# Sparse attention and a GELU layer on one core: the three local jobs of a tile share their score step and their value step

## The chip, the core and the metric

The kernel runs on one core of a Trainium2 chip. The metric is the device time of one execution in microseconds (us). The core's engines are named as the profile names them: PE multiplies matrices (PEld loads its weights), DVE does elementwise work and reductions, ACT does activations and copies, POOL fills and builds masks, SP issues the DMAs. All five run side by side, each through a list of its own, and wait for each other by semaphores.

## The reference

Attention over 8 batches, 8 heads, 576 positions and 64 channels; the first four heads see a window of 32 positions (local), the last four see every 32nd position (strided). Its output, laid out as 4608 tokens of 512 channels, goes through a layer of width 2048 with GELU.

```python
scores = scale * np.matmul(q, k.transpose(0, 1, 3, 2))
rel = pos[:, None] - pos[None, :]
mask_local = (rel >= 0) & (rel < stride)                   # heads 0-3, stride 32
mask_strided = (rel >= 0) & (pos[None, :] % stride == pos[:, None] % stride)   # heads 4-7
attn = softmax(np.where(mask, scores, -1e9))
x = (attn @ v).transpose(0, 2, 1, 3).reshape(B * S, H * D)  # 4608 x 512
h = x @ w_in                                                # 512 x 2048
out = (0.5 * h * (1 + erf(h / sqrt(2)))) @ w_out            # 2048 x 512
```

## The kernel before

**Tiles and steps.** The tokens are cut into 12 tiles of 384, and the layer's width into 16 pieces of 128 (`NF`). A step n handles one piece of one tile: tile n // 16, piece n % 16, 192 steps in all. In a step `ffn_h(n)` does 12 matmuls of 128x384 into one of two PSUM banks `H` (lines L598, L599, L600: each operand is a high and a low part, and three of the four products are taken); `ffn_g(n)` applies GELU on ACT (L607), casts to `gh` on ACT (L609) and subtracts on DVE to get `gl` (L611); `ffn_o(n - 2)` does the 9 matmuls of 128x512 of the step two before (L637, L638, L639) into the banks `O0`, `O1`, `O2`. With two `H` banks, the matmuls H of step n + 2 can begin only when `gl` of step n is done.

**Where x comes from.** The x of a tile (`xh`, `xl`) must be complete when its first step begins. Half of its channels come from the strided heads, worked almost wholly on DVE: products with row sums (L473), a small softmax, then multiply-adds (L515) and a transpose (L523). The other half come from the local heads, in jobs of 128 tokens and four heads, three to a tile (`JPT`). Jobs 0 to 5 (tiles 0 and 1) run in the opening, written out as the list `START`, along with the loading and splitting of the weights and the steps 0 to 15. Jobs 6 to 35 are `band_job`s, and this change is about them.

**A band job** is a generator with seven parts:

- part 0, PE: the scores, 16 matmuls in tiles of 64x32 of the array (L287; 32 records in a trace), half into a PSUM bank `S0`, half into `S1`
- part 1, DVE: mask and row extreme of each of four heads (L301) into a buffer `P`, of which there are two
- part 2, ACT: four exponentials with row sums (L305) into a buffer `PT`
- part 3, DVE and SP: sum, reciprocal, product and 32x32 transpose (L308 to L311), then 8 DMAs that put the blocks into one of three `band` tiles (L316)
- part 4, PE: the values, 8 matmuls in tiles of 96x64 (L324; 16 records in a trace) into a bank `X`
- parts 5 and 6, ACT and DVE: `xh` (L231) and `xl` (L233), then the load of the queries and keys of the job three later

**What sets the order.** In the main loop (steps 16 to 191 and what follows) the order of PE and ACT is the written one, as `step(n)` calls the parts. The orders of DVE, SP and POOL are laid down when the program is built, by the scheduling layer's own reckoning of when rows become ready; on the chip they are then fixed. `PULSES` is a table of 31 steps: 16, 20, 24, then for each later tile three steps (four before, two after and seven after the start of the tile ahead of it), and a last one. At a pulse the values of the job before and the scores of this job stand together, ahead of the step's matmuls H; part 2 follows one step later and part 3 two steps later.

## Time and profile before

| | |
|---|---|
| runs, us | 904.08, 905.25, 905.47 (median 905.25) |
| profiled execution, us | 902.33 |
| its span, first to last instruction, us | 900.6 |
| mean granted clock of TensorE | 0.982 |
| busy, share of the span | PE 97%, PEld 86%, DVE 80%, ACT 49%, POOL 2% |

The profile is one execution seen by the hardware profiler. Its groups give a line's instructions with their busy time and mean duration; its timeline gives instructions in order of time, like ones merged (x16 is sixteen of them, from the first one's start to the last one's end); in brackets stands how long the engine sat idle before it and what ended that. Matmuls overlap, so the pace of PE is read from start to start, not from durations.

### The profile page before, as it was taken

The page shows a single profiled execution, that of the slowest core. Times are in us where ns is not written, and L with a number is a line of the kernel's source. Part 1 is how long each engine was busy: PE and PEld are TensorE (multiplying, and loading weights), DVE is VectorE, ACT ScalarE, POOL GpSimd, SP SyncE. Part 2 cuts the span into 40 slices and gives each one's busy share as a digit, 9 for nine tenths or more (in the row PEclk, how much of TensorE's full clock was granted, in tenths as well). Part 3 has the DMA queues.
Part 4 walks back from the last instruction along what each step waited for, and adds up shares of the span by engine and source line. Part 5 has one row for each costly group of instructions (what it writes and reads, how often), then busy time and mean ns, then how long its engine had stood idle before and what let it go on. Part 6 is the DMA issues. An engine that isn't in the chain of part 4 may idle for free.

```text
span 900.6 us, 19161 instructions
## 1 busy us (share of the span) xinstructions
PE 869.3 (97%) x5948; PEld 772.4 (86%) x5948; DVE 716.2 (80%) x4894; ACT 443.5 (49%) x969; POOL 16.4 (2%) x86
## 2 busy tenths in 40 slices
PE   5599979999999999999999999999999999999998
PEld 4488868888888898888888888888888888889997
DVE  6899988787898899986998996988969899475110
ACT  6899643534544455445544445445453544443222
POOL 4000000000000000000000000000000000000000
PEclk9699998999999999999999999999999999999999
DMA  9992111312112112212121121113112200100001
GB/s 319 361 360 74 51 57 36 101 46 75 30 60 66 31 57 74 75 58 65 30 77 63 57 78 61 32 57 110 32 30 88 70 7 17 59 7 0 36 1 36
DMA packets 33399, 66.27 MB, mean 74 GB/s; under 512 B 6416, under 2 KB 15376, under 8 KB 31248
## 3 DMA queue, kind: packets, MB, share of 16 engines
q1 hardware_dynamic: 33296, 65.04, 22.2%
q8 instruction: 47, 0.77, 0.4%
q14 instruction: 56, 0.46, 0.2%
HBM read 51.64 MB, written 9.44 MB: 68 GB/s over the span
## 4 chain that ended last, share of the span: by engine, by line
PE 92%; ACT 3%; DMA 3%; SPq 1%; issue 0%; DVE 0%
PE H L598 15%; PE O L639 15%; PE O L638 15%; PE H L600 15%; PE H L599 14%; PE O L637 14%; PE X_L L324 2%; DMA ws<-in_w_dram 2%; PE S_L L287 1%; DMA vl<-in_vl_dram 1%; ACT w L160 1%; ACT ws L152 1%; ACT ws L146 0%; SPq L316 0%; ACT L607 0%
## 5 line engine op out<-in xcount | busy, mean ns | idle before, releaser
L607 ACT ACTIVATE H<-H 128x384 f32<-128x384 f32 x192 | 91.3, 476 | 374.5 <-PE H L600 347.3
L598 PE MATMUL H<-xh,w 128*128 128x384 f32 x768 | 264.3, 344 | 4.1 <-DVE gl L611 2.9
L599 PE MATMUL H<-xl,w 128*128 128x384 f32 x768 | 259.8, 338 | 0.7 <-DVE xl L233 0.7
L600 PE MATMUL H<-xh,w 128*128 128x384 f32 x768 | 260.4, 339 | 0.0
L515 DVE SCALAR_TENSOR_TENSOR acc<-sv,sc,acc 128x64 f32<-128x64 f32 x1158 | 248.3, 276 | 0.7
L639 PE MATMUL O<-w,gl 128*128 128x512 f32 x576 | 228.5, 397 | 0.0
L638 PE MATMUL O<-w,gh 128*128 128x512 f32 x576 | 227.8, 396 | 0.0
L637 PE MATMUL O<-w,gh 128*128 128x512 f32 x576 | 225.1, 391 | 0.0
L473 DVE CUSTOM_DVE_ANT_0 junk<-sq,sk 128x64 f32<-128x64 f32 x1290 | 204.3, 219 | 2.1 <-DMA sk<-in_ks_dram 2.1
L611 DVE TENSOR_TENSOR gl<-H,gh 128x384 fp32r<-128x384 f32 x192 | 105.6, 551 | 110.3 <-ACT gh L609 110.2
L598 PEld LDWEIGHTS H<-xh,w 128*128 128x128 f32 x768 | 145.4, 189 | 15.1 <-DVE gl L611 3.8
L599 PEld LDWEIGHTS H<-xl,w 128*128 128x128 f32 x768 | 145.6, 190 | 7.6 <-DVE xl L233 1.1
L600 PEld LDWEIGHTS H<-xh,w 128*128 128x128 f32 x768 | 145.5, 189 | 0.0
L639 PEld LDWEIGHTS O<-w,gl 128*128 128x128 f32 x576 | 108.3, 188 | 23.3
L638 PEld LDWEIGHTS O<-w,gh 128*128 128x128 f32 x576 | 108.4, 188 | 18.3
L637 PEld LDWEIGHTS O<-w,gh 128*128 128x128 f32 x576 | 108.7, 189 | 17.6
L473 DVE DVE_READ_ACCUMULATOR2_ANT sc<- 128x1 f32 x1290 | 106.4, 82 | 0.0
L609 ACT CAST gh<-H 128x384 fp32r<-128x384 f32 x192 | 92.2, 480 | 6.0
L607 ACT ACT_TABLE_LOAD x41 | 52.6, 1283 | 0.9 <-issue 0.2
L483 ACT ACT_TABLE_LOAD x35 | 44.9, 1283 | 0.6
L305 ACT ACTIVATE PT_L<-P_L,nm_L 128x64 f32<-128x64 f32 x120 | 39.9, 333 | 0.0
L231 ACT CAST xh<-X_L 128x256 fp32r<-128x256 f32 x30 | 11.2, 372 | 38.9 <-PE X_L L324 38.7
(106 smaller groups left out, 522.8 us busy)
## 6 DMA issues: line engine op xcount, KB each, us to landing
ws<-in_w_dram SPq DMA_DIRECT2D x16, 1024.0 KB, 14.8
qk<-in_qk_dram SPq DMA_DIRECT2D x36, 320.0 KB, 3.9
out_dram<-ob SPq DMA_DIRECT2D x34, 256.0 KB, 2.7
vl<-in_vl_dram SPq DMA_DIRECT2D x36, 192.0 KB, 2.8
sk<-in_ks_dram SPq DMA_DIRECT2D x8, 576.0 KB, 4.5
sv<-in_vs_dram SPq DMA_DIRECT2D x8, 576.0 KB, 3.8
band<-PT_L SPq DMA_DIRECT2D x240, 16.0 KB, 1.8
sq<-in_qs_dram SPq DMA_DIRECT2D x4, 576.0 KB, 3.6
```

Of the source, the lines that this page charges most:

```text
L473: nc.vector.tensor_tensor_reduce(junk, sq[vi, "q"][:, r0 + r, :], sq[vi, "k"][:, c, :], 1.0, 0.0, ALU.mult, ALU.add, ss[u][:, r, c:c + 1])
L483: exps.append((u, lambda: nc.scalar.activation(s, s, AF.Exp, scale=SC)))
L515: nc.vector.scalar_tensor_tensor(acc[:, r, :], sq[vi, "v"][:, c, :], wgt, acc[:, r, :], ALU.mult, ALU.add)
L598: nc.tensor.matmul(hp, w1[f][:, 0, c, :], xh[:, c, :], start=(c == 0), stop=False)
L599: nc.tensor.matmul(hp, w1[f][:, 0, c, :], xl[:, c, :], start=False, stop=False)
L600: nc.tensor.matmul(hp, w1[f][:, 1, c, :], xh[:, c, :], start=False, stop=(c == NC - 1))
L607: nc.scalar.activation(hp, hp, AF.Gelu)
L609: nc.scalar.copy(gh, hp)
L611: nc.vector.tensor_tensor(gl, hp, gh.bitcast(F32), ALU.subtract)
L637: nc.tensor.matmul(o, gh[:, sl], w2[f][:, 0, :], start=(f == 0), stop=False)
L638: nc.tensor.matmul(o, gh[:, sl], w2[f][:, 1, :], start=False, stop=False)
L639: nc.tensor.matmul(o, gl[:, sl], w2[f][:, 0, :], start=False, stop=(f == NF - 1))
```

## The change

The three band jobs of a tile take their scores in one visit of PE and their values in another. `SCORES` and `VALUES` are steps after the start of the tile ahead: at step 2 the parts 0 of the three jobs, then their parts 1; at step 12 their parts 4, then 5 and 6. The softmaxes stay apart: part 2 and part 3 of job i come 2i + 1 and 2i + 2 steps after the scores. So there are ten visits for scores (18, 34, ... 162) and ten for values (28, 44, ... 172), where there were 31 pulses. The three jobs' scores lie side by side in one pair of banks (128 columns each), and their values in `X` (jobs 0 and 1) and in the bank `S0` (job 2). Nothing else is changed; the buffers `P` and `PT` stay two each, the `band` tiles three.

```diff
-    def band_job(x, bt):
+    def band_job(x, bt, sx):
         QB = STRIDE
-        s = [ps_a.tile([P, DM], F32, name=f"S{j}_L{x}", tag=f"S{j}") for j in range(2)]
+        i = x % JPT
+        if i == 0:
+            sx["s"] = [ps_a.tile([P, DM], F32, name=f"S{j}_L{x}", tag=f"S{j}") for j in range(2)]
+        s = [t[:, i * P:(i + 1) * P] for t in sx["s"]]
...
-        xp = ps_a.tile([P, DM], F32, name=f"X_L{x}", tag="X")
-        xv = xp[:, 0:N2 * P].rearrange("p (r q) -> p r q", r=N2)
+        if i % 2 == 0:
+            sx["x"] = ps_a.tile([P, DM], F32, name=f"X_L{x}", tag="X" if i == 0 else "S0")
+        xv = sx["x"][:, i % 2 * N2 * P:(i % 2 + 1) * N2 * P].rearrange("p (r q) -> p r q", r=N2)
...
-    PULSES = [NB, NB + 4, NB + 8] + [ready[t - 1] + o for t in range(3, NTILE) for o in (-4, 2, 7)]
-    PULSES.append(ready[NTILE - 1] - 4)
+    SCORES, VALUES = 2, 12
+    score_at = {ready[t - 1] + SCORES: t for t in range(2, NTILE)}
+    value_at = {ready[t - 1] + VALUES: t for t in range(2, NTILE)}
...
+    def visit(n):
+        for i in range(JPT):
+            for d, p in ((1, 2), (2, 3)):
+                t = score_at.get(n - 2 * i - d)
+                if t is not None:
+                    if p == 2:
+                        flush_exps(NU)
+                    part(t * JPT + i, p)
+        if n in score_at:
+            for p in (0, 1):
+                for i in range(JPT):
+                    part(score_at[n] * JPT + i, p)
+        if n in value_at:
+            for ps in ((4,), (5, 6)):
+                for i in range(JPT):
+                    part(value_at[n] * JPT + i, *ps)
...
     def step(n):
...
-        before(n)
-        pulse(n)
+        visit(n)
```

The lists of the two built programs show what moves. Names carry the job or the step: `S0_L7` is bank S0 of job 7, `H_20` and `gl_34` belong to steps 20 and 34. Lines from L320 on stand four higher after the change, those between L280 and L317 three.

On PE, before, at step 20 (the second pulse): the end of O of step 17, the values of job 6, and the first scores of job 7.

```order
L638 MATMUL O_1_2_1644<-w_1_584,gh_17_1589 128x512
L639 MATMUL O_1_2_1644<-w_1_584,gl_17_1590 128x512
L324 MATMUL X_L6_1723<-band_1443,vl_6_775 64x64 x8
L287 MATMUL S0_L7_1734<-qk_7_1092 32x64
L287 MATMUL S1_L7_1735<-qk_7_1092 32x64
```

On PE after the change, at step 28: the values of jobs 6, 7 and 8 in one visit, with no scores behind them. The scores of the three (48 rows that alternate between S0 and S1) stand at step 18, right behind H of step 17.

```order
L642 MATMUL O_1_2_1678<-w_9_920,gh_25_2141 128x512
L643 MATMUL O_1_2_1678<-w_9_920,gl_25_2142 128x512
L328 MATMUL X_L6_2254<-band_1443,vl_6_775 64x64 x8
L328 MATMUL X_L6_2254<-band_1443,vl_7_1068 64x64 x8
L328 MATMUL X_L8_2275<-band_1443,vl_8_1347 64x64 x8
L602 MATMUL H_28_2312<-xh_1_826,w_12_1111 128x384
```

The first values have moved from step 20, four steps after their job's scores, to step 28, ten steps after; the pair of values and scores in one visit is gone.

On DVE after the change, behind `gl` of the score step 34: the masks of jobs 9 and 10 stand ahead of these rows, those of job 11 (the third of its tile) here.

```order
L615 TENSOR_TENSOR gl_34_2708<-H_34_2694,gh_34_2707 128x384
L519 SCALAR_TENSOR_TENSOR acc_9_2519<-sv_4_1441,sc_9_1962,acc_9_2519 128x64
L503 TENSOR_REDUCE z_10_96<-sc_10_2352 128x2
L519 SCALAR_TENSOR_TENSOR acc_9_2519<-sv_4_1441,sc_9_1962,acc_9_2519 128x64
L509 TENSOR_SCALAR z_10_96<-z_10_96 128x2
L519 SCALAR_TENSOR_TENSOR acc_9_2519<-sv_4_1441,sc_9_1962,acc_9_2519 128x64
L510 RECIPROCAL z_10_96<-z_10_96 128x2
L304 ISA P_L11_2670,nm_L11_2672<-S0_L9_2602,bmaskNone_89 128x64
```

With two buffers `P`, the third job's masks write the first job's buffer, so they wait for the first job's exponentials on ACT, which stand there behind GELU and cast of step 34; before, the masks of a job waited for its scores alone.

On DVE after the change, at the head of what stands between `gl` of step 133 and that of step 134 (36 rows in all, 23 of L519 by their counts, 9 products L477, a job's product and transpose, one transpose L527, one `xl`).

```order
L615 TENSOR_TENSOR gl_133_9216<-H_133_9202,gh_133_9215 128x384
L519 SCALAR_TENSOR_TENSOR acc_32_9444<-sv_9_8622,sc_32_8859,acc_32_9444 128x64 x2
L313 TENSOR_TENSOR PT_L28_8993<-PT_L28_8993,rs_L28_8996 128x256
L519 SCALAR_TENSOR_TENSOR acc_31_9038<-sv_9_8622,sc_31_8624,acc_31_9038 128x64 x3
L519 SCALAR_TENSOR_TENSOR acc_32_9444<-sv_9_8622,sc_32_8859,acc_32_9444 128x64 x2
L314 STREAM_TRANSPOSE PT_L28_8993<-PT_L28_8993 128x256
```

The softmax of job 28, the second of tile 9, has come here from another step, and two units of strided work stand interleaved with it.

## The prediction

> **What bounds the kernel now.** I read the page first: which engine is busy, and which makes up the chain that ended last.

> ```profile
> span 900.6 us, 19161 instructions
> PE 869.3 (97%) x5948; PEld 772.4 (86%) x5948; DVE 716.2 (80%) x4894; ACT 443.5 (49%) x969; POOL 16.4 (2%) x86
> PE 92%; ACT 3%; DMA 3%; SPq 1%; issue 0%; DVE 0%
> ```

> PE holds 92% of the chain. A busy PE says little of its pace, so I go to the timeline of PE and read starts. First a bare step, then a pulse of two jobs:

> ```profile
> 305.83 0.33 PE L598 MATMUL H<-xh,w 128*128 128x384 f32 x1
> 306.00 0.34 PE L599 MATMUL H<-xl,w 128*128 128x384 f32 x1
> 309.79 0.39 PE L639 MATMUL O<-w,gl 128*128 128x512 f32 x1
> 310.02 0.33 PE L598 MATMUL H<-xh,w 128*128 128x384 f32 x1
> ...
> 313.97 0.40 PE L639 MATMUL O<-w,gl 128*128 128x512 f32 x1
> 314.30 0.69 PE L324 MATMUL X_L<-band,vl 96*64 96x64 f32 x16
> 314.92 0.45 PE L287 MATMUL S_L<-qk 64*32 64x64 f32 x32
> 315.30 0.44 PE L598 MATMUL H<-xh,w 128*128 128x384 f32 x1
> 315.58 0.34 PE L599 MATMUL H<-xl,w 128*128 128x384 f32 x1
> ```

> A step takes 4.19 us (305.83 to 310.02); H follows H after 0.17, and anything follows O after 0.23. At the pulse 0.33 goes by before the values, 0.62 from them to the scores, 0.38 from these to H, and 0.28 to the second H: 1.61, where 0.40 would stand without it. **A pulse costs PE 1.21 us.** The same figures stand at every pulse from 155 us on, and nothing else slows PE there. The stretch before holds three extra losses:

> ```profile
> 108.76 0.39 PE L637 MATMUL O<-w,gh 128*128 128x512 f32 x1
> ...
> 111.06 0.39 PE L638 MATMUL O<-w,gh 128*128 128x512 f32 x1
> 111.38 0.30 PE L287 MATMUL S_L<-qk 64*32 64x64 f32 x2
> 111.61 0.50 PE L639 MATMUL O<-w,gl 128*128 128x512 f32 x1
> ...
> 116.66 0.44 PE L598 MATMUL H<-xh,w 128*128 128x384 f32 x1
> ...
> 124.88 0.40 PE L639 MATMUL O<-w,gl 128*128 128x512 f32 x1
> 125.85 0.45 PE L598 MATMUL H<-xh,w 128*128 128x384 f32 x1 [0.58 <-DVE gl L611]
> 126.14 0.34 PE L599 MATMUL H<-xl,w 128*128 128x384 f32 x1
> ...
> 129.92 0.40 PE L639 MATMUL O<-w,gl 128*128 128x512 f32 x1
> 132.37 0.34 PE L324 MATMUL X_L<-band,vl 96*64 96x64 f32 x4 [2.05 <-DMA band<-PT_L]
> 134.76 0.91 PE L324 MATMUL X_L<-band,vl 96*64 96x64 f32 x12 [2.05 <-DMA band<-PT_L]
> 136.21 0.69 PE L598 MATMUL H<-xh,w 128*128 128x384 f32 x1
> ```

> - The first job's scores come in four pieces among the matmuls O (one shows at 111.38). From 108.76 to 116.66 stand 27 O, 27 x 0.23 = 6.21 of 7.90 us; with the 0.11 that the second H loses at every return (0.28 less 0.17): **1.80**.
> - At 125.85 H waits for `gl`: 0.97 instead of 0.23, and 0.29 instead of 0.17: **0.86**.
> - At step 20 the first values wait twice for the band DMAs. From 129.92 to 136.21 go 6.29 us, against 1.33 at the pulse above: 4.96. Then the clock falls, as windows of the four steps behind this pulse and behind the next show (each from the first H to the last O):

> ```profile
> core 0: us, PE busy (x) PEld busy (x) DVE busy (x) ACT busy (x) POOL busy (x), PEclk, DMA share, GB/s
> ...
> 136.20:155.00 18.80, 18.80 (x92) 17.16 (x84) 16.91 (x150) 8.25 (x20) 0.13 (x1) 0.87 0.14 37
> 156.30:172.90 16.60, 16.60 (x97) 15.08 (x84) 14.07 (x84) 8.08 (x20) 0.11 (x1) 1.00 0.34 112
> ```

> The granted clock was 0.87 instead of 1.00 and the four steps took 2.20 more: with the wait **7.16**.

> [...]

> **The sum before.** 29 pulses with both kinds at 1.21 make 35.1; the last, values alone, 1.21 - 0.38 = 0.83; the three losses 9.8. PE spends **45.7 us** on band jobs and what they provoke, over its bare steps.

> **The change part by part.** *The visits of PE.* In a group, the starts span its length less one matmul's time. L324 lasts 0.69 us with 222 ns for one, so 0.47 over 15 intervals, 31 ns each; L287 0.45 with 216 ns, 0.23 over 31, 7.5 ns each (medians from the lines' own rows):

> ```profile
> L287 PE MATMUL S_L<-qk x960: 216/216/313, 111.4 to 786.7; 64*32 64x64 f32 x192
> ...
> L324 PE MATMUL X_L<-band,vl x480: 222/222/366, 132.4 to 808.5; 96*64 96x64 f32 x160
> ```

> A visit of scores for three jobs is 0.33 + 0.38 for the first, 64 more at 7.5 ns = 0.48, 0.28 at the end, less 0.40: 1.07. A visit of values is 0.33 + 0.62, 32 more at 31 ns = 1.00, 0.28, less 0.40: 1.83. Together 2.90 a tile, 29.0 for ten tiles. The other bound charges each job the whole 0.38 or 0.62, with no gain inside a visit: 1.35 + 2.07 = 3.42, or 34.2. I take 29.0, since the rows inside a group are the nearest to what is added.

> [...]

> *The start.* The first scores stand behind H of step 17 in one piece, so the 1.80 goes into the visit already counted. The order between H and O there changes too; H of step 18 no longer follows two H at once, so `gl` has O and a visit more time, and the 0.86 goes. The first values stand eight steps later. The last of the three softmaxes ends in step 24, its 8 DMAs were issued in 5.37 us (row below), and four steps of 4.19 are left for them. So the 7.16 goes, clock included. What is late next is `gl` on DVE in steps 16 to 21.

> ```profile
> 105.80 0.22 DVE L473 CUSTOM_DVE_ANT_0 junk<-sq,sk 128x64 f32<-128x64 f32 x1
> ...
> 105.95 0.22 DVE L473 CUSTOM_DVE_ANT_0 junk<-sq,sk 128x64 f32<-128x64 f32 x1
> ...
> 111.24 0.55 DVE L611 TENSOR_TENSOR gl<-H,gh 128x384 fp32r<-128x384 f32 x1
> ...
> 128.03 5.37 SPq L316 DMA_DIRECT2D band<-PT_L  x8
> ...
> 303.71 2.63 DVE L515 SCALAR_TENSOR_TENSOR acc<-sv,sc,acc 128x64 f32<-128x64 f32 x13
> ```

> On DVE a product takes 0.15 from start to start, a multiply-add 2.63 / 13 = 0.20. At such paces the list has 5.4, 3.4, 4.6 and 4.9 us of rows from `gl` of step 15 (111.24) to those of steps 16, 17, 18 and 19, which brings the last to 129.5; three short waits on ACT, some 0.6 each, to 131.3. PE, from 108.76 through 27 O, two H and the visit, reaches H of step 18 at 120.2 and H of step 21 at 132.8. So `gl` of step 19 ends about 0.9 us before it is needed, the others earlier. I cost this at nothing; if the cover is gone by more than 2 us, the clock goes too.

> *The third masks, and step 134.* The slack of `gl` in the long run of steps is this (two rows of the timeline, two groups):

> ```profile
> 304.45 0.48 ACT L609 CAST gh<-H 128x384 fp32r<-128x384 f32 x1
> 306.26 0.55 DVE L611 TENSOR_TENSOR gl<-H,gh 128x384 fp32r<-128x384 f32 x1
> ...
> L305 ACT ACTIVATE PT_L<-P_L,nm_L 128x64 f32<-128x64 f32 x120 | 39.9, 333 | 0.0
> L483 ACT ACT_TABLE_LOAD x35 | 44.9, 1283 | 0.6
> ```

> `gh` of step 57 was done at 304.93, `gl` began 1.33 later, and H of step 59 began at 310.02; `gl` could have begun 4.5 us after `gh`. The third job's masks now wait for four exponentials behind `gh`: a table load 1.28, a strided exponential, four at 0.33, some 2.8 us. Queued behind them on DVE are the rest of that step's strided rows and the next `gl`. Masks and rows come to about 3.4 us, so that `gl` begins 6.2 after this `gh`, 2.0 after its own, which comes a step of 4.19 later: inside 4.5. Cost nothing. Between `gl` of steps 133 and 134, though, the list has 23 multiply-adds at 0.20, 9 products at 0.15, and four larger rows beside `gl`: 7.6 us for a step of 4.19. That adds 3.4 to the lateness with which `gl` of step 133 begins. With 1.33, as above, it is 4.7; with twice that, three steps behind a score visit, 6.1; against 4.5. H of step 136 then waits 0.2 to 1.6 us; I charge 0.8 (bounds 0 and 1.6). The list of ACT has 14 more table loads (96 for 82), 18 us, some in front of a GELU; ACT is 49% busy, and 1.28 us of delay is inside the same slack. The loads of queries and keys wait on SP for the scores and come sixteen steps before they are needed; they are not on the path.

> After: 29.0 + 0.8 = 29.8; **gain 45.7 - 29.8 = 15.9 us**. The profiled execution, 902.33 (2.92 below the median), would take 886.4; carried over to the median of the runs, 905.25 - 15.9 = **889.4**.

> **Rivals.**

> - *Each job keeps its own drain* inside a visit: 34.2 instead of 29.0, 894.6. For it: only groups of one job are traced. Against: pieces of 31 and 7.5 ns do not know of jobs. 0.10.
> - *The start stays late*: `gl` takes the place of the band DMAs around steps 19 to 21, stalls PE by about 5 us and halves the clock: 889.4 + 7.2 = 896.6. For it: the cover of 0.9 and the 0.58 wait at 125.85. 0.13.
> - *DVE late in many tiles*, some 0.6 us at each score visit: 895.4. For it DVE's 93.88 busy of 100 us in its fullest stretch; against it 4.5 us of slack. 0.10.

> ```profile
> 300.00:400.00 100.00, 100.00 (x671) 89.27 (x670) 93.88 (x662) 46.64 (x106) 0.64 (x5) 1.00 0.17 55
> ```

> - *Slower*: DVE stands at the third job's masks until the first job's exponentials are through, and `gl` and with it H stop in all ten score steps. It decides from `gl` 4.5 us after `gh`; to eat 15.9 it must be 1.6 us past that each time, so 2.0 would give 889.4 + 20 = 909.4. By the sum above `gl` is some 2 us late, not 6.1. 0.04.
> - *No change*: the gains of the start show in the profiled execution only and drains stay too: about 904. 0.03.

> **How the numbers follow.** The forecast holds 0.60, with its own range 886.6 to 892.2 (0.2 us a tile either way in the visits, 0 to 1.6 at step 136). The range of 8 in 10 takes in the drains, the late DVE and the late start: 886.6 to 896.6. A measurement of this kernel tells about 0.2%, 1.8 us, from no change: faster 0.92, same 0.04, slower 0.04.

> **What would show it.** Right: ten stretches of 1.2 us from the last O to H with 96 score records in them, and ten of 1.95 with 48 value records; a clock of 1.00 from 110 us on; no wait for the band DMAs; at most a short wait of H for `gl` near step 136. Wrong: values that start a new 0.15 us gap at every job; PE waiting for `gl` at 130 us with the clock below 1; waits of H for `gl` that recur every sixteen steps; waits of the masks for ACT above 4 us.

## The result, and the profile after

| | before | after |
|---|---|---|
| first set of runs, median (lowest to highest), us | 905.15 (904.08 to 905.47), 4 runs | 889.27 (887.55 to 891.09), 4 runs |
| ratio, 95% interval | | 0.9827 [0.9803, 0.9850] |
| second set, median, us | 902.71, 17 runs | 889.88 (887.86 to 892.37), 6 runs |
| ratio, 95% interval | | 0.9862 [0.9838, 0.9886] |
| profiled execution, us | 902.33 | 890.20 |
| its span, us | 900.6 | 888.4 |

The kernel became faster by 15.9 us in the first set and by 12.8 us in the second. The page of the kernel after, with its clock row over 40 slices of the span:

```profile
span 888.4 us, 19181 instructions
PE 860.2 (97%) x5948; PEld 771.0 (87%) x5948; DVE 714.1 (80%) x4894; ACT 461.2 (52%) x983; POOL 16.3 (2%) x86
PEclk9699999999999999999999999999999999999999
PE 91%; DVE 4%; DMA 3%; ACT 1%; SPq 0%; issue 0%; DVEq 0%
```

PE still makes the chain, and its clock is 0.9 or more in every slice after the second. The stretch that held the start's losses, as a window of the kernel after (per engine the busy time, then the granted clock, DMA's share and GB/s):

```profile
core 0: us, PE busy (x) PEld busy (x) DVE busy (x) ACT busy (x) POOL busy (x), PEclk, DMA share, GB/s
110.00:155.00 45.00, 45.00 (x317) 40.42 (x316) 43.82 (x411) 27.78 (x63) 0.28 (x2) 1.00 0.19 60
```

No gap of PE and a clock of 1.00 stand there. The timeline of the kernel after, in order: a values visit, a score visit, and what goes on near step 134 on DVE, ACT and PE:

```profile
162.94 0.40 PE L643 MATMUL O<-w,gl 128*128 128x512 f32 x1
163.27 1.62 PE L328 MATMUL X_L<-band,vl 96*64 96x64 f32 x48
164.82 0.44 PE L602 MATMUL H<-xh,w 128*128 128x384 f32 x1
165.10 0.33 PE L603 MATMUL H<-xl,w 128*128 128x384 f32 x1
...
189.81 0.40 PE L643 MATMUL O<-w,gl 128*128 128x512 f32 x1
190.14 1.17 PE L290 MATMUL S_L<-qk 64*32 64x64 f32 x96
191.24 0.45 PE L602 MATMUL H<-xh,w 128*128 128x384 f32 x1
...
629.58 0.57 DVE L615 TENSOR_TENSOR gl<-H,gh 128x384 fp32r<-128x384 f32 x1
...
634.73 0.41 ACT L231 CAST xh<-xs 128x256 fp32r<-128x256 f32 x1 [6.40 <-DVE xs L527]
...
635.54 0.48 ACT L613 CAST gh<-H 128x384 fp32r<-128x384 f32 x1
...
636.50 0.40 PE L643 MATMUL O<-w,gl 128*128 128x512 f32 x1
...
637.19 0.57 DVE L615 TENSOR_TENSOR gl<-H,gh 128x384 fp32r<-128x384 f32 x1
...
637.82 0.44 PE L602 MATMUL H<-xh,w 128*128 128x384 f32 x1 [0.93 <-DVE gl L615]
```

A values visit loses 1.88 + 0.28 - 0.40 = 1.76 us (forecast 1.83), a score visit 1.43 + 0.28 - 0.40 = 1.31 (forecast 1.07): 3.07 a tile instead of 2.90. H of step 136 waits once: 1.32 + 0.28 - 0.40 = 1.20 (forecast 0 to 1.6, charged 0.8).

To compare whole runs, all excess of a start over the bare pace (0.17 us behind H, 0.23 behind O; unrounded 0.174 and 0.231) that is larger than 0.05 us is added up, from the first O behind H of step 15 to the last O. This is **PE's loss**: 45.5 us before, which the prediction put at 45.7, and 31.9 after, which it put at 29.8. The gain of PE's starts is 13.6 us, not 15.9. From outside, the first O to the last took 896.29 - 108.76 = 787.5 us before and 884.13 - 109.62 = 774.5 after: 13.0 less (the other 0.6 us lies in excesses under 0.05). So the gain that the prediction summed was 2.3 us too large, and that 889.4 lies 0.1 us from the first set's median is luck. The profiled execution after took 890.2, not the forecast 886.4. Of these 3.8 us, 2.3 are the smaller gain of PE's starts, 0.6 the excesses under 0.05, and 0.9 stand ahead of the first O counted (109.62 after, 108.76 before), ahead of every visit that the change moves.

### The profile page after: what moved, and what is told of

It reads as the page before. It is cut to its first block, busy times and chain, and to the rows that moved or that the text cites. A ratio compares the mean times of both kernels' runs of the same rounds, so it can differ in the third digit from the quotient of the medians.

```text
span 888.4 us, 19181 instructions
## 1 busy us (share of the span) xinstructions
PE 860.2 (97%) x5948; PEld 771.0 (87%) x5948; DVE 714.1 (80%) x4894; ACT 461.2 (52%) x983; POOL 16.3 (2%) x86
## 4 chain that ended last, share of the span: by engine, by line
PE 91%; DVE 4%; DMA 3%; ACT 1%; SPq 0%; issue 0%; DVEq 0%
PE H L602 15%; PE O L642 15%; PE H L604 15%; PE O L643 15%; PE H L603 15%; PE O L641 14%; DMA ws<-in_w_dram 2%; PE X_L L328 2%; DMA vl<-in_vl_dram 1%; PE S_L L290 1%; DVE acc L519 1%; DVE junk L477 1%; DVE ws L154 0%; DVE w L164 0%; DVE ws L156 0%
## 5 line engine op out<-in xcount | busy, mean ns | idle before, releaser
L611 ACT ACTIVATE H<-H 128x384 f32<-128x384 f32 x192 | 91.4, 476 | 352.8 <-PE H L604 315.6
L519 DVE SCALAR_TENSOR_TENSOR acc<-sv,sc,acc 128x64 f32<-128x64 f32 x1158 | 258.3, 287 | 0.6
L477 DVE CUSTOM_DVE_ANT_0 junk<-sq,sk 128x64 f32<-128x64 f32 x1290 | 214.5, 228 | 6.3 <-DMA sk<-in_ks_dram 6.2
L615 DVE TENSOR_TENSOR gl<-H,gh 128x384 fp32r<-128x384 f32 x192 | 107.4, 560 | 113.1 <-ACT gh L613 112.1
L477 DVE DVE_READ_ACCUMULATOR2_ANT sc<- 128x1 f32 x1290 | 118.8, 92 | 0.0
L611 ACT ACT_TABLE_LOAD x48 | 61.6, 1283 | 1.1 <-issue 0.3
L487 ACT ACT_TABLE_LOAD x35 | 44.9, 1283 | 0.6
L517 DVE TENSOR_SCALAR acc<-sv,sc 128x64 f32<-128x64 f32 x132 | 25.9, 253 | 0.5 <-DMA sv<-in_vs_dram 0.2
```

The costliest lines, as they stand in the source:

```text
L477: nc.vector.tensor_tensor_reduce(junk, sq[vi, "q"][:, r0 + r, :], sq[vi, "k"][:, c, :], 1.0, 0.0, ALU.mult, ALU.add, ss[u][:, r, c:c + 1])
L487: exps.append((u, lambda: nc.scalar.activation(s, s, AF.Exp, scale=SC)))
L519: nc.vector.scalar_tensor_tensor(acc[:, r, :], sq[vi, "v"][:, c, :], wgt, acc[:, r, :], ALU.mult, ALU.add)
L611: nc.scalar.activation(hp, hp, AF.Gelu)
L615: nc.vector.tensor_tensor(gl, hp, gh.bitcast(F32), ALU.subtract)
```

## The experiments

Each kernel is compared with runs of the kernel before on the same chip; "loss" is PE's loss as above. It leaves out what stands ahead of the first O counted, and that stretch is not the same everywhere: in the profiled executions this O begins between 108.24 us (third masks free) and 112.38 us (first values late).

| kernel | median, us | ratio to before, 95% | loss, us |
|---|---|---|---|
| first values late | 896.34 | 0.9933 [0.9910, 0.9955] | 38.6 |
| clean start | 894.63 | 0.9917 [0.9897, 0.9936] | 37.7 |
| old start, shared visits | 900.03 | 0.9971 [0.9959, 0.9984] | 41.7 |
| scores single | 896.43 | 0.9924 [0.9897, 0.9951] | 37.1 |
| scores 1 + 2 | 892.68 | 0.9890 [0.9866, 0.9914] | 35.2 |
| scores mixed | 889.87 | 0.9857 [0.9834, 0.9879] | 31.9 |
| values single | 898.74 | 0.9942 [0.9918, 0.9965] | 38.8 |
| third masks free | 889.55 | 0.9848 [0.9828, 0.9869] | 31.9 |
| xh behind | 889.04 | 0.9842 [0.9827, 0.9858] | 31.2 |
| one visit | 901.40 | 0.9972 [0.9957, 0.9986] | 41.4 |
| one visit, xh behind | 894.53 | 0.9900 [0.9878, 0.9921] | 37.1 |

### The changed kernel again

> The changed kernel once more, unedited, for a tighter interval and as the yardstick of the other kernels of this set. If the gain is the 15.9 us that the prediction summed, the median lies near 889.4 and the ratio near 0.982. The two profiled executions differ by 12.1 us only, and the itemized losses of PE by 13.6 (45.5 before, 31.9 after); if these are the truer figures, the median lies 12 to 14 us below that of before, 891 to 893.

889.88 for 902.71: 12.8 less, loss 31.9. As a difference, this set bears out the second statement and the first set the first (the medians of before differ too, by 2.4 us). The intervals of the two ratios overlap from 0.9838 to 0.9850 only, and the traces' 13.6 us (0.985) stands at the edge of that.

### First values late

The kernel before, with the first values taken out of the pulse of step 20.

```diff
-            part(x - 1, 4)
+            if x - 1 != J0:
+                part(x - 1, 4)
             part(x, 0)
-            part(x - 1, 5, 6)
+            if x - 1 != J0:
+                part(x - 1, 5, 6)
             part(x, 1)
+        if n == NB + 7:
+            part(J0, 4, 5, 6)
```

> The kernel before, with one edit: the values of job 6 stand by themselves at step 23 and no longer at step 20; all else is as before, so the visits of PE keep their old form. My theory: the two waits for the band DMAs (4.96 us) and the fall of the clock behind them (2.20 us) go; the visit at step 20 keeps only scores (0.59 us by 0.33 + 0.38 + 0.28 - 0.40), the one at step 23 only values (0.83), together 0.21 more than one pulse at 1.21. So 6.95 us less than before, near 898.2. Rival 1: the wait goes, but the clock falls in these steps all the same: 4.75 less, near 900.4. Rival 2: the wait stood in the profiled execution only, or the product gl takes its place: no gain, near 905.

Timeline of this kernel, the scores at step 20 and the values at step 23, and its window over these steps:

```profile
133.56 0.40 PE L639 MATMUL O<-w,gl 128*128 128x512 f32 x1
133.89 0.45 PE L287 MATMUL S_L<-qk 64*32 64x64 f32 x32
134.27 0.44 PE L598 MATMUL H<-xh,w 128*128 128x384 f32 x1
...
146.69 0.40 PE L639 MATMUL O<-w,gl 128*128 128x512 f32 x1
147.01 0.69 PE L324 MATMUL X_L<-band,vl 96*64 96x64 f32 x16
147.63 0.44 PE L598 MATMUL H<-xh,w 128*128 128x384 f32 x1
```

```profile
133.80:150.00 16.20, 16.20 (x125) 14.50 (x125) 16.20 (x158) 7.79 (x19) 0.00 (x0) 1.00 0.14 35
```

Scores alone lose 0.71 + 0.28 - 0.40 = 0.59, values alone 0.94 + 0.28 - 0.40 = 0.82. The waits are gone and the clock is 1.00. The loss fell by 6.9 us (forecast 6.95), the median by 6.4: the start's 7.16 were real, clock included. The interval of the ratio alone, 4.1 to 8.1 us, would not tell this from the 4.75 of rival 1; the clock of 1.00 in the window does.

### Clean start

The same edit, and the first scores two steps later.

```diff
-    PULSES = [NB, NB + 4, NB + 8] + [ready[t - 1] + o for t in range(3, NTILE) for o in (-4, 2, 7)]
+    PULSES = [NB + 2, NB + 4, NB + 8] + [ready[t - 1] + o for t in range(3, NTILE) for o in (-4, 2, 7)]
```

> The edit of the kernel before (values of job 6 at step 23), and also the first scores at step 18 instead of 16. My theory: the scores no longer cut up the matmuls O behind H of step 15 (1.80 us less, 0.59 for a visit of scores at step 18) and H of step 18 no longer waits for gl (0.86 less): 6.95 + 1.80 - 0.59 + 0.86 = 9.0 us less than before, near 896.1. Rival: the masks and the softmax of two jobs, now two steps apart, hold gl up on DVE and PE waits in steps 20 to 24: less than 7 us gained, above 898.

The four pieces and the wait of step 18 went, but at step 24 the values of job 7 meet their band DMA. PE, with less lost ahead, is there 2.1 us sooner (37.6 us behind the first O counted; 39.6 in the kernel first values late), while the issue of these DMAs begins 0.6 us later (32.61 for 32.05) and lasts until 147.32, with the visit at 147.34:

```profile
147.02 0.40 PE L639 MATMUL O<-w,gl 128*128 128x512 f32 x1
147.34 0.34 PE L324 MATMUL X_L<-band,vl 96*64 96x64 f32 x4
148.65 0.57 PE L324 MATMUL X_L<-band,vl 96*64 96x64 f32 x12 [0.97 <-DMA band<-PT_L]
...
149.53 0.44 PE L598 MATMUL H<-xh,w 128*128 128x384 f32 x1
```

This visit loses 2.51 + 0.28 - 0.40 = 2.39 instead of 1.21. So 9.0 - 1.2 = 7.8 us were to be had; the loss fell by 7.8, the median by 8.1.

### Old start, shared visits

The changed kernel with jobs 6 to 8 on the pulses 16, 20, 24 and 28.

```diff
...
-    score_at = {ready[t - 1] + SCORES: t for t in range(2, NTILE)}
-    value_at = {ready[t - 1] + VALUES: t for t in range(2, NTILE)}
+    score_at = {ready[t - 1] + SCORES: t for t in range(3, NTILE)}
+    value_at = {ready[t - 1] + VALUES: t for t in range(3, NTILE)}
...
+        first = {NB: 2 * JPT, NB + 4: 2 * JPT + 1, NB + 8: 2 * JPT + 2}
...
+        if n in (NB + 4, NB + 8, NB + 12):
+            part(first[n - 4], 4)
+        if n in first:
+            part(first[n], 0)
...
```

> The changed kernel, with the three jobs of the first tile (6 to 8) put back on the pulses 16, 20, 24 and 28, each with scores and values as before; the nine later tiles keep the shared visits. My theory: the start's losses come back (1.80, 0.86 and 7.16 us) with two pulses at 1.21 and values alone at 0.83, 13.1 in all, and one tile's two visits (1.31 + 1.75 = 3.06 measured) go: 10.0 us more than the changed kernel, 899 to 901. So what the shared visits of nine tiles are worth by themselves is 9 x (3 x 1.21 - 3.06) = 5.1 us. Rival: the visits are worth more than PE's starts show, and the start less: 896 or lower.

The band waits are back in this kernel's timeline:

```profile
132.84 0.34 PE L327 MATMUL X_L<-band,vl 96*64 96x64 f32 x4 [1.96 <-DMA band<-PT_L]
135.35 0.91 PE L327 MATMUL X_L<-band,vl 96*64 96x64 f32 x12 [2.17 <-DMA band<-PT_L]
```

It is 10.2 us slower than the changed kernel in the same set (forecast 10.0), and 2.7 faster than before. The loss fell by 3.8 from before: nine tiles at 3 x 1.21 - 3.07 = 0.56 are 5.0, less the stall of 1.2 near step 136, which stands here too. **Some 10 us of the gain come from the start, some 4 from all the shared visits, the stall near step 136 taken off.**

### Scores single, scores 1 + 2, scores mixed

The changed kernel with its scores split over three visits (scores single, the first diff), over two (scores 1 + 2; the same lines go), or in another order within one (scores mixed: half jobs in turn).

```diff
-        if n in score_at:
-            for p in (0, 1):
-                for i in range(JPT):
-                    part(score_at[n] * JPT + i, p)
+        for i in range(JPT):
+            if n - 2 * i in score_at:
+                part(score_at[n - 2 * i] * JPT + i, 0, 1)
```

```diff
+        if n in score_at:
+            part(score_at[n] * JPT, 0, 1)
+        if n - 2 in score_at:
+            for p in (0, 1):
+                for i in (1, 2):
+                    part(score_at[n - 2] * JPT + i, p)
```

```diff
         for h in range(0, HL, 2):
...
-        yield
+            yield
...
+            for _ in range(2):
+                for x in xs:
+                    next(local[x][0])
```

> The changed kernel, with the scores of the three jobs of a tile taken in three visits, two steps apart (steps 2, 4 and 6 behind the start of the tile ahead); the values still share one. Nothing else moves on PE. A visit of one job's scores alone lost 0.48 + 0.11 = 0.59 us in the kernel before with the late first values. My theory (entry and exit are paid per visit): 3 x 0.59 = 1.77 a tile for 1.31, 4.6 us more than the changed kernel, near 894.5; PE shows 32 records a visit, 7.5 ns apart. Rival (each job keeps its own drain within a shared visit, so a split costs nothing): 890.

> The changed kernel, with the scores of job 0 in a visit of its own at step 2 and those of jobs 1 and 2 in one visit at step 4. In the changed kernel the first job's 32 records start 7.5 ns apart, those of the second and third 12 and 11 ns apart, with one hole of 0.056 behind the 33rd. Theory A (PE's instructions come from a stock that the wait for the matmuls O fills, about 32 records with their weights, and then arrive at some 11 ns): the visit of two slows down behind its own 32nd record too and loses 0.59 + 0.03 + 0.41 = 1.0 us; 1.6 a tile, 3 us more than the changed kernel, near 893. Theory B (only the third of a group, or only the second and third job's data are slow): other places of the hole; with 7.5 ns throughout the visit of two would lose 0.83, 1.42 a tile, 1 us more.

> The changed kernel, with the score matmuls of one visit in another order: the first half (two heads) of job 0, of job 1, of job 2, then the second halves. The tiles of the array follow each other as before. Theory A (a stock of about 32 records): the hole and the slower pace stay behind the 32nd record, which is now the end of job 1's first half; the visit loses 1.3 us as before, the time stays at 890. Theory B (the second and third job's own queries and keys or columns are slow): the slow pace begins behind record 16, with job 1, and is back at 7.5 ns when job 0's second half comes, behind record 48.

The timeline of scores 1 + 2, the visit of jobs 1 and 2; its second row holds what a window of the first 0.31 us of the visit shows, the records that begin in it:

```profile
269.02 0.40 PE L643 MATMUL O<-w,gl 128*128 128x512 f32 x1
269.35 0.48 PE L290 MATMUL S_L<-qk 64*32 64x64 f32 x33
269.35 0.86 PE L290 MATMUL S_L<-qk 64*32 64x64 f32 x64
270.14 0.44 PE L602 MATMUL H<-xh,w 128*128 128x384 f32 x1
```

The same window of the changed kernel, and of scores mixed:

```profile
190.14 0.48 PE L290 MATMUL S_L<-qk 64*32 64x64 f32 x33
```

```profile
329.85 0.48 PE L290 MATMUL S_L<-qk 64*32 64x64 f32 x33
329.85 1.17 PE L290 MATMUL S_L<-qk 64*32 64x64 f32 x96
```

A visit of one job loses 0.59, of two 1.12 + 0.28 - 0.40 = 1.00, of three 1.31. In all three kernels 33 records begin within 0.48 - 0.21 = 0.27 us, some 8 ns apart; a hole follows (0.056 in the changed kernel), and with it the other 63 of 96 take 1.17 - 0.48 = 0.69, 11 ns each. The place of the hole does not move when the first 33 records are another job's (1 + 2) or the first halves of jobs 0 and 1 (mixed): it goes by the count from the head of the scores, as theory A said, and theory B falls. (In the kernel one visit, further down, 48 value records stand ahead of the scores in the same visit, and the break still comes behind the 33rd score record.) Theory A's stock of PE's instructions was the author's guess from this count: no row shows a stock, its size or what fills it. What the runs show is the 33, in these three kernels and in one visit.

Scores single took 6.6 us more than scores mixed in the same set (which equals the changed kernel), scores 1 + 2 took 2.8 more (forecast 4.6 and 3). Their losses are 5.2 and 3.3 larger: 4.6 and 2.7 from the visits, the rest from the stall near step 136, which grew from 1.2 to 1.7 and 1.9. What the 6.6 has beyond 5.2 is no loss of the visits: the profiled executions lie 6.7 apart, and 1.9 of that stands ahead of the first O counted (111.17 for 109.25).

### Values single

```diff
-        if n in value_at:
-            for ps in ((4,), (5, 6)):
-                for i in range(JPT):
-                    part(value_at[n] * JPT + i, *ps)
+        for i in range(JPT):
+            if n - i in value_at:
+                part(value_at[n - i] * JPT + i, 4, 5, 6)
```

> The changed kernel, with the values of the three jobs in three visits, one step apart (steps 12, 13 and 14); the scores still share one. A visit of one job's values alone lost 0.71 + 0.11 = 0.82 us in the kernel before with the late first values. My theory: 3 x 0.82 = 2.46 a tile for 1.75, 7 us more than the changed kernel, near 897. Rival (each job keeps its own drain in the shared visit): 890.

Its timeline, the last O ahead of one of the three visits and the first H behind it (0.94 apart; the second H follows after 0.28, as everywhere):

```profile
235.72 0.40 PE L643 MATMUL O<-w,gl 128*128 128x512 f32 x1
...
236.66 0.44 PE L602 MATMUL H<-xh,w 128*128 128x384 f32 x1
```

A visit loses 0.94 + 0.28 - 0.40 = 0.82, three 2.46 for 1.76. The loss grew by 6.9; the median is 8.9 above that of scores mixed, 2 us more than the starts show. The profiled executions lie 9.5 apart, and 2.4 of that stands ahead of the first O counted (111.66 for 109.25), far ahead of the first values. Within a shared visit no job keeps a drain of its own (the whole 0.62 from its values to what follows them): three lose 1.76, where 0.62 for each would make 2.07.

### Third masks free, xh behind

The first gives job 2 of each tile a buffer `P3` of its own. The second issues the strided heads' cast and subtraction behind GELU and cast of their step.

```diff
-        p1 = lpool.tile([P, 4 * LK], F32, name=f"P_L{x}", tag="P", bufs=2)
+        p1 = (lpool.tile([P, 8 * QB], F32, name=f"P_L{x}", tag="P3", bufs=1) if i == 2 else
+              lpool.tile([P, 4 * LK], F32, name=f"P_L{x}", tag="P", bufs=2))
```

```diff
-        while splits and n >= xfree[splits[0][0]]:
-            for _ in splits.pop(0)[1]():
-                pass
+        due = len([x for x in splits if n >= xfree[x[0]]])
...
             for _ in ffn_g(n):
                 pass
+        for _ in range(due):
+            for _ in splits.pop(0)[1]():
+                pass
```

> The changed kernel, with a buffer P of its own for the third job of a tile, so that its masks no longer wait for the first job's exponentials; in the order of DVE some rows move with it. My theory (that wait costs PE nothing in nine tiles, since gl has 4.5 us of slack): no change in the visits of PE, no change of time but for the stall of H of step 136 (1.2 us), whose 7.6 us of rows between gl of steps 133 and 134 stay (37 rows for 36); the start of that list moves, so 0 to 2 us there; 889 to 891. Rival (the wait of the masks does cost, hidden in many small delays of H): 2 us or more less, and H starts earlier at the score steps.

> The changed kernel, with the cast xh and the subtraction xl of the strided heads issued behind GELU and cast of their step instead of ahead of them; gl of step 134 then stands 8 rows behind that of step 133 on DVE instead of 36, and GELU of step 134 no longer stands behind a cast that waits 6.4 us for DVE's transpose. My theory (the stall of H of step 136 comes from these rows on DVE): it goes, or moves to the next gl, which now has 40 rows ahead of it, and is smaller there (0 to 0.6 us); 0.6 to 1.2 us less than the changed kernel, near 889. Rival (the stall follows the backlog of the strided work in these steps, wherever it stands): H waits as long a step later, no gain.

The wait that the third masks had, among the waits of DVE in the changed kernel (in all, times, longest):

```profile
DVE P_L L304 <- ACT PT_L L308: 1.4, 3, 0.5
```

1.4 us in three places was all, on an engine with slack. Without it the loss is 31.9, as in the changed kernel; H of step 136 still waits, in its timeline:

```profile
634.96 0.40 PE L644 MATMUL O<-w,gl 128*128 128x512 f32 x1
636.30 0.44 PE L603 MATMUL H<-xh,w 128*128 128x384 f32 x1 [0.95 <-DVE gl L616]
```

With xh behind, the wait moved to H of step 137 and shrank (timeline: PE, DVE and ACT):

```profile
634.60 0.41 ACT L231 CAST xh<-xs 128x256 fp32r<-128x256 f32 x1 [3.48 <-DVE xs L527]
...
640.09 0.56 DVE L615 TENSOR_TENSOR gl<-H,gh 128x384 fp32r<-128x384 f32 x1 [1.07 <-ACT gh L613]
...
640.16 0.40 PE L643 MATMUL O<-w,gl 128*128 128x512 f32 x1
640.70 0.44 PE L602 MATMUL H<-xh,w 128*128 128x384 f32 x1
```

0.54 + 0.28 - 0.40 = 0.42 is left of 1.20, and it has another cause: DVE stands idle 1.07 for `gh`, as ACT waited 3.48 us at xh. Loss 31.2, the lowest of all; 889.04 is the lowest median too, but no run here tells it from the changed kernel's 889.3 to 889.9.

### One visit, without and with xh behind

The values of a tile and the scores of the next in one visit (step 12); the third job's values go to columns 384 to 511 of S0 and S1. The second kernel also has the edit xh behind, placed behind the copies `ob`.

```diff
...
-    score_at = {ready[t - 1] + SCORES: t for t in range(2, NTILE)}
+    score_at = {NB + SCORES if t == 2 else ready[t - 2] + VALUES: t for t in range(2, NTILE)}
...
+        for at, ps in ((value_at, (4,)), (score_at, (0,)), (value_at, (5, 6)), (score_at, (1,))):
+            if n in at:
+                for i in range(JPT):
+                    part(at[n] * JPT + i, *ps)
```

> The changed kernel, with the values of a tile and the scores of the next tile in one visit at step 12: scores move six steps ahead, the third job's values go to the free quarters of the banks S0 and S1, and the loads of queries and keys follow the scores. A pulse with both kinds lost 1.20 us where values and scores in visits of their own lose 0.82 + 0.59 = 1.41. My theory (the entry of a visit is paid once for both kinds): 0.21 x 9 = 1.9 us less on PE, near 888, if DVE's order, which moves with the masks, brings no new wait of H for gl. Rival (a stock of PE's instructions that the long values use up): the scores start slow from their first record and lose 0.3 us more a visit, no gain. Rival: new waits of H for gl near steps 130 to 140, some 1 to 5 us, 890 to 893.

> The kernel with one visit for a tile's values and the next tile's scores, with the cast xh and the subtraction xl of the strided heads issued at the end of a step, behind GELU, cast and the copies ob. In that kernel each of nine visits lost 2.86 us where two visits lose 3.06, but O waited 4.74 us for ob behind an xh that waited 6.1 us for DVE's transpose, H waited 1.6 us near 658 us, and PE stood 2.68 us with nothing that the profile shows; the clock fell behind two of these. My theory: the waits that start at xh go (4.74 with some 1.7 of clock, and 1.2 or more of the wait near 658): 8 us less, near 893 if the stop of 2.68 (with 1.8 of clock) comes again, near 889 if it doesn't. Rival (the backlog on DVE comes back at another gl): less than 4 us gained, above 897.

The first kernel's timeline, a visit (its second row is what a window up to 233.86 shows, the first 0.30 us of the scores), and the two largest gaps behind the opening:

```profile
231.68 0.40 PE L655 MATMUL O<-w,gl 128*128 128x512 f32 x1
...
233.56 0.48 PE L293 MATMUL S_L<-qk 64*32 64x64 f32 x33
...
234.66 0.45 PE L614 MATMUL H<-xh,w 128*128 128x384 f32 x1
...
307.21 0.21 PE L293 MATMUL S_L<-qk 64*32 64x64 f32 x1 [2.68 <-issue]
...
761.63 0.79 PE L653 MATMUL O<-w,gh 128*128 128x512 f32 x1 [4.74 <-ACT ob L660]
```

A visit loses 2.98 + 0.28 - 0.40 = 2.86 for 3.07, as forecast, and 1.9 us were saved so. The 33 score records again begin within 0.27 us, behind 48 value records, so the rival of a stock that the values use up falls. The 1.9 were lost several times over: 901.40, with a loss of 41.4 for 31.9.

With xh behind, the 4.74 and the slow clock behind it (0.63 from 761.50 to 766.00) went, 6.5 us by PE's starts. A new wait of H for gl near 175 us took 2.0 back, and the wait near 658 shrank from 1.6 to 1.3 only, so the loss fell by 4.3. The medians differ by 6.9, but they come from two sets, and the first kernel's runs spread from 897.98 to 902.92; the forecast 8 is not shown. The second kernel's waits of PE:

```profile
PE H L614 <- DVE gl L627: 3.6, 2, 1.8
PE S_L L293 <- issue: 2.8, 1, 2.8
```

The stop ahead of a visit's last score record came again in the same visit; its cause stays open.

## Why the prediction was right, and where it was not

**The sum before** held: 45.5 us for 45.7. The pulse at 1.21 and the three losses of the start were read from starts, and the kernels first values late, clean start and old start moved them by what the terms say (6.9 for 6.95; 7.8 for 9.0 less a new wait of 1.2; 10.2 for 10.0).

**The start** went whole, clock included. Its cover was larger than the 0.9 us that the prediction gave: in the trace `gl` of step 19 ended at 132.03 and H of step 21 began at 133.87, 1.8 us later.

**The visits of PE** came out 3.07 a tile for 2.90. The term that was mis-sized is "64 more at 7.5 ns = 0.48" in the score visit: they took 0.72, since a group of 32, the only one that the trace of before had, does not show what happens to the 33rd record. That is 2.4 us over ten tiles. "32 more at 31 ns" in the values visit was 0.07 too dear, 0.7 us back: their 48 records keep one pace, (1.62 - 0.22) / 47 = 30 ns, from first to last.

**The third masks** cost nothing, as forecast: they waited 1.4 us in all.

**Step 136** stalled where the list of DVE said, by 1.20 us for a charged 0.8. The rows between `gl` of steps 133 and 134 took 637.19 - 629.58 = 7.6 us as counted. The prediction missed a second route: xh on ACT, ahead of GELU of step 134, waited 6.40 us for DVE's transpose, so that `gh` was done only at 636.02. Here DVE was later still; in xh behind, this route set what was left.

**The rivals.** Drains kept by each job: refuted by values single and scores single, since a split would then be free, and the loss grew by 6.9 and 5.2. By the bound a values visit would lose 2.07 and a score visit 1.35; they lose 1.76 and 1.31, the scores near it only by their slower pace behind the 33rd record. The late start and the slower case did not come. Late DVE in many tiles: only step 136.

**The gain.** 13.6 us by PE's starts for 15.9: 2.4 too much in the scores, 0.4 in the stall, 0.7 too little in the values, 0.2 in the sum before. The two sets' 15.9 and 12.8 lie on both sides; why they differ by 3 us stays open. The 4 us by which the profiled executions differ ahead of the first O counted would be enough for it, but no row shows it for these runs.

## What to carry to other kernels

Count a switch between kinds of matmul per visit, not per job (here 0.59 us for a score visit of one job, 0.31 to 0.41 for each further one), and trust the pace inside a group only as far as the longest group in the trace (here 32 scores at 7.5 ns; the 63 behind the 33rd took 11 each). All the shared visits were worth less than one early dependency: moving the first values behind their band DMAs brought 7 us (the whole start 10), all the shared visits some 4. Put nothing that waits for a far row ahead of the row that the bottleneck needs next: in the changed kernel xh waited 6.40 us on ACT with GELU of step 134 written behind it, and in one visit xh waited 6.10 and O then 4.74 for `ob`.

## What was not expected of the hardware

The granted clock fell behind some short gaps of PE and not behind others. The window behind the gap of 2.68 in the kernel one visit, the one behind the gap of 0.97 in clean start, and a gap of 1.82 in the kernel one visit, xh behind, with its window:

```profile
307.20:311.30 4.10, 4.09 (x14) 3.95 (x14) 3.54 (x46) 0.27 (x1) 0.00 (x0) 0.58 0.66 210
```

```profile
149.50:154.00 4.50, 4.50 (x38) 4.08 (x24) 4.50 (x58) 2.16 (x4) 0.00 (x0) 1.00 0.41 122
```

```profile
175.33 0.44 PE L614 MATMUL H<-xh,w 128*128 128x384 f32 x1 [1.82 <-DVE gl L627]
...
175.30:180.00 4.70, 4.67 (x23) 3.98 (x24) 4.70 (x32) 2.24 (x4) 0.00 (x0) 1.00 0.02 5
```

The gap of 2.68 us had 0.58 behind it, those of 0.97 and 1.82 had 1.00. In the opening of the changed kernel one gap of 2.28 us, up to 45.18, had 1.00 behind it to 46.00, 0.59 and 0.56 in the windows from there to 48.00 and to 50.00, and 1.00 from 50.00 to 60.00; one of 2.22, up to 8.94, had 1.00 in the windows from 9.00 to 14.00. So the length of one gap did not decide it alone, and no run here tells where the fall begins. Behind the two gaps of 2.05 us in the kernel before the clock was 0.50 from 136.20 to 140.20, and in old start, behind 1.96 and 2.17, it was 0.50 from 136.80 to 141.00. The two of each pair stand 0.34 us apart, so they do not tell whether one of them would have been enough; the prediction's 2 us of lost cover, behind which the clock goes too, was an estimate from the first pair.
